# The last pair of heads of an attention and expert kernel: separate buffers, parallel copies, and slots scaled in the activation

## The chip, the cores and the metric

The kernel runs on one core of a Trainium2 chip. The metric is device time in microseconds (us), as the median of several runs. Five engines are spoken of: PE (TensorE: matrix multiply, and transposes by an identity matrix), DVE (VectorE), ACT (ScalarE), POOL (GpSimd) and SP (SyncE, which issues the transfers). Each runs its own instructions in the order written and waits for others by semaphores.

## The reference

For 4 batches and 8 heads of 768 tokens and 64 values, an attention with a window and a few global keys:

```
scores = q @ k.T / 8 - slope[h] * dist          # 96 last keys, and 8 global keys
a = exp(scores - max); a = a / (a.sum(-1) + 1e-9)
x = a @ v                                       # -> 3072 tokens x 512
logits = x @ phi                                # 3072 x 32 slots
d = exp(logits - logits.max(0)); d = d / (d.sum(0) + 1e-9)
slot_input = d.T @ x                            # 32 slots x 512
h = relu(slot_input[e] @ w1[e])                 # 8 experts, 4 slots each, 512 -> 1024
slot_out = h @ w2[e]                            # 1024 -> 512
c = softmax(logits, over slots); out = c @ slot_out
```

Dividing a slot by its sum of `d` is a scale of one row of `slot_input`. Since `relu(s * y) = s * relu(y)` for positive s, it can stand before the first expert product or in the activation behind it.

## The kernel before

The attention is done in 16 units: 4 batches, and in each 4 pairs of heads. For a unit PE makes scores, DVE adds the bias and takes a maximum, ACT takes the exponential and a float16 high part (`w_hi`), POOL and DVE the low part (`w_lo`), PE multiplies by the values (`values`, L609, 39 products a head). DVE then adds a small constant to the sums (`ev_sums`, L622), takes reciprocals (`ev_recs`, L628) and multiplies (`ev_mul`, L634, one a head). PE transposes the result (`tr`, L646: four blocks for k = 0, three for k = 1), and ACT or DVE copies the transposed parts out of PSUM (`tr_copy`, L651; `tr_copy_dve`, L655). With two units transposed, `logits` (L676) multiplies by `phi`. The last unit is 15; its own logits are made in `logits2`.

The order in which the instructions stand on every engine is a table written out by hand, `ORDER`: a list of steps with unit and head. There is no planner; what one row of the table issues stands behind what the rows ahead of it issued.

At the end of each batch the logits strip is added up (`logits_all`, L693), the running maximum over batches is updated (`strip_max`, L710 and L711) and the exponential `ex` is taken on ACT (`strip_exp`, L716). Batches 0 to 2 then turn `ex` into token rows (L732, L745), and `dispatch` (L755) multiplies it with x; `dispatch_sum` (L766) adds the product to the slot sums `sacc`.

For batch 3 that is `last_dispatch`, the stretch between the attention and the expert layer: `ex` is turned (L732) into one PSUM tile and copied (L745) into `dn`; DVE finds a factor per strip (L799 to L802, ACT L803); 14 products (L755); a product with ones (L815) for the sums; DVE divides (L816 to L818) and adds (L766); PE brings the 128 strip rows of `sacc` together into slots (L827, two pairs), and DVE copies them into `sl` (L96). Between these stand short products that nothing reads (`warm`, L542).

The expert layer begins with `hidden` (L101): 128 products of 512 columns into two banks, `hp[0]` and `hp[1]`, each step being 4 products for one block c of 128 inputs and one half n, then ACT's Relu (L119, L124). `project` (L154) and `combine` (L206) follow, whose outputs ACT and DVE copy (L211) and SP sends off (L212). Behind `hidden` SP loads the expert weights that had no room (L404), into buffers which `hidden` has read.

Two heads of a unit share one PSUM tile of two banks, `xx`, and `sc[0]` and `sc[1]` are two more such tiles; instructions on one tile wait for each other as written by the tile library.

## Time and profile before

| | us |
|---|---|
| median of 3 runs | 187.21 (186.58 to 187.63) |
| the profiled execution | 186.55 |
| its span | 184.5 |
| PE busy | 171.4 (93%) |
| DVE busy | 141.3 (77%) |
| ACT busy | 124.8 (68%) |
| POOL busy | 96.8 (52%) |

The profile is of one execution. Its span runs from the first instruction to the last; 2.05 us of the execution lie around it. Busy shares are means over stages: the attention takes the first two thirds, the stretch of `last_dispatch` begins at about 128 us, `hidden` at 134.98 us, and the last output is issued at about 178 us.

### The profile page before, as it was taken

How to read it: one execution, taken by the hardware profiler on the slowest of the kernel's cores; microseconds unless marked ns; L12 is line 12 of the kernel's file. 1: busy time of each engine (PE TensorE's matmuls, PEld its weight loads, DVE VectorE, ACT ScalarE, POOL GpSimd, SP SyncE). 2: the span in 40 equal slices, each digit the busy share in tenths (PEclk: the TensorE clock that was granted, in tenths of full speed). 3: DMA queues.
4: the chain of work that ended last, by engine and by line, in shares of the span. 5: the costliest groups of instructions: out<-in, count | busy, mean ns of one | idle time of the engine just before them, and what ended most of it. 6: DMA issues, size and time to landing. Idle time of an engine off the chain costs nothing. (4 is left out here: it accounts for less than half of the span.)

```text
span 184.5 us, 6749 instructions
## 1 busy us (share of the span) xinstructions
PE 171.4 (93%) x2811; PEld 126.4 (69%) x2811; DVE 141.3 (77%) x378; ACT 124.8 (68%) x160; POOL 96.8 (52%) x128
## 2 busy tenths in 40 slices
PE   8999899999999999999999998998899999999740
PEld 2567689797878878989788896874443256677530
DVE  5999999999999899999999999886687203345330
ACT  3399989999989999979999999942302110344330
POOL 6826689859789489797998978720010000000000
PEclk9999999999999999999999999999999999999965
DMA  6999999979989954889885599999999999979792
GB/s 197 414 413 368 413 401 380 367 220 339 378 318 361 386 195 179 313 314 358 294 338 216 167 291 400 383 380 421 415 359 311 420 401 409 372 274 400 304 362 86
DMA packets 15306, 61.41 MB, mean 333 GB/s; under 512 B 1698, under 2 KB 2850, under 8 KB 13474
## 3 DMA queue, kind: packets, MB, share of 16 engines
q1 hardware_dynamic: 15264, 60.89, 87.8%
q8 instruction: 24, 0.39, 0.8%
q14 instruction: 16, 0.13, 0.2%
q10 hardware_dynamic: 2, 0.00, 0.0%
HBM read 54.59 MB, written 6.29 MB: 330 GB/s over the span
## 5 line engine op out<-in xcount | busy, mean ns | idle before, releaser
L592 POOL TENSOR_TENSOR ph<-tb,ph 128x432 f16<-128x432 f32 x83 | 85.7, 1063 | 19.2 <-ACT ph L585 18.0
L582 ACT ACTIVATE tb<-tb,nb 128x1296 f32<-128x1296 f32 x32 | 43.7, 1374 | 0.9 <-DVE nb L578 0.8
L609 PEld LDWEIGHTS <-ph 128*128 128x128 f16 x1248 | 40.6, 97 | 4.5 <-issue 3.2
L609 PE MATMUL x<-v,ph 128*128 128x65 f16 (+1 forms) x1248 | 43.1, 193 | 0.6 <-DVE xmax L634 0.3
L585 ACT CAST ph<-tb 128x1296 f16<-128x1296 f32 x32 | 40.6, 1271 | 2.5 <-PE x L609 0.7
L557 PE MATMUL sc<-raw 64*128 64x216 f32 (+1 forms) x392 | 40.8, 340 | 0.0
L557 PEld LDWEIGHTS sc<-raw 64*128 64x128 f32 x392 | 32.3, 186 | 6.0 <-issue 3.5
L634 DVE CUSTOM_DVE_ANT_1 xn<-x,rc 120x448 f32<-120x448 f32 x32 | 18.8, 621 | 2.1 <-PE m L755 1.6
L566 DVE CUSTOM_DVE_ANT_1 tb<-sc,tt,mx 128x864 f32<-128x864 f32 x16 | 17.8, 1114 | 1.1 <-DVE mx L566 0.7
L535 DVE SCALAR_TENSOR_TENSOR v<-vt,v 128x896 f16<-128x896 f32 x14 | 16.0, 1144 | 0.0
L646 PE MATMUL m<-ident,xn 120*128 120x120 f32 x105 | 15.6, 276 | 0.2 <-DVE xmax L634 0.2
L646 PEld LDWEIGHTS m<-ident,xn 120*128 120x128 f32 x105 | 10.7, 140 | 2.7 <-issue 1.2
L101 PE MATMUL hp<-wp,sl 128*32 128x512 f32 x80 | 10.7, 593 | 0.0
L206 PE MATMUL cp<-sos,ct 32*128 32x128 f32 (+1 forms) x116 | 8.6, 343 | 1.3 <-DVE sos L193 1.1
L566 DVE CUSTOM_DVE_ANT_1 tb<-sc,xtt,mx 128x864 f32<-128x864 f32 x8 | 8.9, 1114 | 0.4 <-DVE mx L566 0.2
L592 DVE TENSOR_TENSOR ph<-tb,ph 128x432 f16<-128x432 f32 x13 | 9.1, 721 | 0.0
L566 DVE CUSTOM_DVE_ANT_1 tb<-sc,xta,mx 128x864 f32<-128x864 f32 x8 | 8.9, 1110 | 0.2
L528 ACT ACTIVATE v<-vt 128x896 f16<-128x896 f32 x9 | 8.6, 951 | 0.1
L566 DVE CUSTOM_DVE_ANT_1 tb<-sc,tt 128x864 f32<-128x864 f32 x8 | 8.4, 1051 | 0.0
L154 PE MATMUL o<-wp,ht 128*32 128x128 f32 x256 | 8.2, 275 | 0.0
L884 POOL MEMSET ht<- 128x536 f32 x1 | 0.5, 544 | 14.0 <-PE ld L827 14.0
L206 PEld LDWEIGHTS cp<-sos,ct 32*128 32x128 f32 x116 | 5.9, 192 | 2.6 <-DVE sos L193 1.5
(220 smaller groups left out, 283.4 us busy)
## 6 DMA issues: line engine op xcount, KB each, us to landing
raw<-in_qk_dram SPq DMA_DIRECT2D x14, 832.0 KB, 6.2
wp<-in_w_dram SPq DMA_DIRECT2D x10, 1024.0 KB, 8.4
wp<-in_w_dram SPq DMA_DIRECT2D x15, 512.0 KB, 9.3
vt<-in_v_dram SPq DMA_DIRECT2D x14, 448.0 KB, 5.4
tb<-in_w_dram SPq DMA_DIRECT2D x3, 1024.0 KB, 8.6
wp<-in_qk_dram SPq DMA_DIRECT2D x2, 832.0 KB, 9.6
raw<-in_w_dram SPq DMA_DIRECT2D x2, 832.0 KB, 4.6
ph<-in_w_dram SPq DMA_DIRECT2D x2, 768.0 KB, 8.9
```

What stands on the lines that cost most here:

```text
L101: self.nc.tensor.matmul(out=hp[n][32 * s:32 * s + 32, :], lhsT=slv(a, c, s), rhs=w1(4 * a + s, c // 2)[:, (c % 2) * DF + 512 * n:(c % 2) * ...
L206: nc.tensor.matmul(out=cps[b][:, w * h:w * h + w], lhsT=ct[r, P * t:P * t + P], rhs=so[r, f:f + w], start=True, stop=True)
L528: nc.scalar.activation(out=vhi[u % 2][:, :, :, 0:D], in_=vraws(u), func=AF.Copy, scale=V_SC)
L535: nc.vector.scalar_tensor_tensor(out=vlo[k].rearrange("p j i d -> p (j i) d"), in0=vraws(u).rearrange("p j i d -> p (j i) d"), scalar=V_SC ...
L557: nc.tensor.matmul(out=z[:, i, at:at + n], lhsT=r_[r, KCOL[j]:KCOL[j] + KR], rhs=r_[r, KW + KB * j:KW + KB * j + n], start=True, stop=True)
L566: nc.vector.tensor_tensor_reduce(out=tb(u)[:, :, BW * k:BW * k + BW], in0=sc[(3 * u + k) % 2][:, :, 0:BW], in1=table.unit(u % NP, k), scal ...
L582: nc.scalar.activation(out=t, in_=t, func=AF.Exp, bias=nbs[u], scale=T_SC)
L585: nc.scalar.copy(out=blocks(phi_[i])[:, :, 0:QW], in_=tb(u)[:, i].rearrange("p (s c) -> p s c", c=QW))
L592: (engine or nc.gpsimd).tensor_tensor(out=blocks(plo_[i])[:, c, 0:QW], in0=tb(u)[:, i].rearrange("p (s c) -> p s c", c=QW)[:, c], in1=bloc ...
L609: nc.tensor.matmul(out=x[:, (D + 1) * t:(D + 1) * t + d], lhsT=w[:, c:c + P], rhs=vv[:, j, i, 0:d], start=(z == 0), stop=(z == len(ops) - ...
L634: nc.vector.tensor_tensor_reduce(out=xnb[(u // 2) % 3][:, :, c:c + D], in0=xv[:, i, :, 0:D], in1=rcs.pop((u, i)).unsqueeze(2).to_broadcast ...
L646: nc.tensor.transpose(out=m[:, at:at + KB], in_=xnb[(u // 2) % 3][:, t, P * (p % 2):P * (p % 2) + P], identity=ident[0:KB, 0:KB])
```

## The change

The rows of `ORDER` at the end of unit 15 are written in another order, and `LAST_BANKS` gives the last units other PSUM banks: the second head of unit 15 gets a bank of its own in `sc[0]`, is normalised by itself (`ev_sum`, `ev_rec`, `ev_mul`) ahead of the first head, and the two turned parts of unit 15 stand in two tiles, one copied by DVE and one by ACT. Unit 14's turned parts go to the two banks of `sc[1]`. `dispatch_sum` of batch 2 moves behind the copies.

`strip_max` keeps the negative of the maximum, in one instruction. For batch 3 the sum of `ex` is a DVE reduction in place of ACT's accumulator. In `last_dispatch` `ex` is turned into two tiles and copied as two halves ahead of ACT's exponential of the factor; the 14 products stand together; two of the five `warm` calls go. The slots are not divided: `hidden` takes the reciprocal as the Relu's scale (`zn`, one number per row). Slots of the first two blocks are copied by ACT; those of the later two (`put_rest`) are made inside `hidden`, behind its first four products, and with them goes the softmax over slots on DVE.

```diff
-('values', 15, 1), ('dispatch_sum', 11), ('values', 15, 0), ('tr', 14, 1), ('tr_copy', 13, 0), ('tr_copy', 14, 1), ('ev_sums', 15), ('ev_recs', 15),
+('values', 15, 1), ('ev_sum', 15, 1), ('ev_rec', 15, 1), ('ev_mul', 15, 1), ('values', 15, 0), ('tr', 14, 1), ('tr_copy', 13, 0), ('tr', 14, 0),
...
         return view
-    def put_slots(self, sl, m, c0=0, c1=4):
+    def put_slots(self, sl, m, c0=0, c1=4, copy=None):
         n = 4 * (c1 - c0)
         out = bass.AP(tensor=sl.tensor, offset=sl.offset + 8 * 4 * c0, ap=[sl.ap[0], [P + SPE, 2], [8, n], [1, SPE]])
-        self.nc.vector.tensor_copy(out=out, in_=m.rearrange("p (cs a i) -> p a cs i", a=2, i=SPE))
+        (copy or self.nc.vector.tensor_copy)(out=out, in_=m.rearrange("p (cs a i) -> p a cs i", a=2, i=SPE))
     def hidden_part(self, hp, slv, w1, a, c, n):
...
                 start=(a == 0 and c == 0), stop=(a == 1 and c == 3), skip_group_check=True)
-    def hidden(self, ps, slv, w1, hs, ht, freed=(None, None)):
+    def hidden(self, ps, slv, w1, hs, ht, freed=(None, None), scale=1.0, rest=None):
         hp = [ps.tile([P, 512], F32, name="hp", tag="x") for _ in range(2)]
...
                 self.hidden_part(hp, slv, w1, 0, c, n)
+                if c == 0 and n == 0 and rest:
+                    rest()
         if freed[0]:
...
             freed[1]()
-        self.nc.scalar.activation(out=hs[:, 0:512], in_=hp[0], func=AF.Relu)
+        self.nc.scalar.activation(out=hs[:, 0:512], in_=hp[0], func=AF.Relu, scale=scale)
         for c in range(4):
...
             self.hidden_part(hp, slv, w1, 1, c, 1)
-        self.nc.scalar.activation(out=hs[:, 512:1024], in_=hp[1], func=AF.Relu)
+        self.nc.scalar.activation(out=hs[:, 512:1024], in_=hp[1], func=AF.Relu, scale=scale)
     HT = 2 * 32 * 8 + 24
...
     i4 = keep.tile([P, NS], F32, name="i4")
+    by_row = keep.tile([P, NS], F32, name="by_row")
     ones = keep.tile([P, P], F32, name="ones")
...
         nc.gpsimd.tensor_tensor(out=i4, in0=i4, in1=ident[:, 96:128], op=ALU.add)
+        nc.gpsimd.tensor_copy(out=by_row.rearrange("p (s j) -> p s j", s=4), in_=ident.rearrange("p (s r) -> p s r", s=4)[:, :, 0:NS // 4])
         nc.gpsimd.memset(sl, 0.0)
...
         return tbuf[u % 3]
-    LAST_BANKS = {("logits", last): (0, 0), ("tr", last, 0): (1, 0), ("tr", last, 1): (1, 1)}
+    LAST_BANKS = {("tr", last - 1, 1): sc[1][:, 1], ("tr", last - 1, 0): sc[1][:, 0], ("logits", last - 2): sc[0][:, 0],
+                  ("tr", last, 0): xx[:, 1], ("tr", last, 1): sc[1][:, 1], ("logits", last): sc[0][:, 1]}
+    def sums(u, i):
+        return sc[0][:, i] if (u, i) == (last, 1) else xx[:, i]
     def bank(key):
         if key in LAST_BANKS:
-            k, i = LAST_BANKS[key]
-            return sc[k][:, i]
+            return LAST_BANKS[key]
         return psm.tile([P, 512], F32, name="m", tag="m")
...
         vh, vl = vhi[u % 2], vlo[u % 2]
-        x = xx[:, i]
+        x = sums(u, i)
         ops = []
...
     xv = xx[0:KB, :, 0:NJ * (D + 1)].rearrange("p i (t d) -> p i t d", d=D + 1)
+    def by_query(u, i):
+        return sums(u, i)[0:KB, 0:NJ * (D + 1)].rearrange("p (t d) -> p t d", d=D + 1)
     def ev_sum(u, i):
-        nc.vector.tensor_tensor(out=rsall[:, 2 * u + i, :], in0=xv[:, i, :, D], in1=eps, op=ALU.add)
+        nc.vector.tensor_tensor(out=rsall[:, 2 * u + i, :], in0=by_query(u, i)[:, :, D], in1=eps, op=ALU.add)
     def ev_rec(u, i):
...
         nc.vector.tensor_tensor_reduce(
-            out=xnb[(u // 2) % 3][:, :, c:c + D], in0=xv[:, i, :, 0:D], in1=rcs.pop((u, i)).unsqueeze(2).to_broadcast([KB, NJ, D]), scale=1.0,
+            out=xnb[(u // 2) % 3][:, :, c:c + D], in0=by_query(u, i)[:, :, 0:D], in1=rcs.pop((u, i)).unsqueeze(2).to_broadcast([KB, NJ, D]), scale=1.0,
             scalar=-3.0e38, op0=ALU.mult, op1=ALU.max, accum_out=xmax[:, m:m + 1])
...
         if b == 0:
-            nc.vector.tensor_copy(out=new, in_=al[:, 4:5])
+            nc.vector.tensor_scalar(out=new, in0=al[:, 4:5], scalar1=-1.0, scalar2=None, op0=ALU.mult)
         else:
-            nc.vector.tensor_tensor(out=new, in0=al[:, 4:5], in1=old, op=ALU.max)
-        nc.vector.tensor_scalar(out=al[:, 1:2], in0=new, scalar1=-1.0, scalar2=None, op0=ALU.mult)
+            nc.vector.tensor_scalar(out=new, in0=al[:, 4:5], scalar1=-1.0, scalar2=old, op0=ALU.mult, op1=ALU.min)
     @of_b
...
         al = als[b]
-        nc.scalar.activation(out=ex, in_=lsb, func=AF.Exp, bias=al[:, 1:2], accum_out=al[:, 3:4])
+        new, old = state[:, b % 2:b % 2 + 1], state[:, 1 - b % 2:2 - b % 2]
+        if b < B - 1:
+            nc.scalar.activation(out=ex, in_=lsb, func=AF.Exp, bias=new, accum_out=al[:, 3:4])
+        else:
+            nc.scalar.activation(out=ex, in_=lsb, func=AF.Exp, bias=new)
         if b:
-            old = state[:, 1 - b % 2:2 - b % 2]
-            nc.scalar.activation(out=al[:, 0:1], in_=old, func=AF.Exp, bias=al[:, 1:2])
+            nc.scalar.activation(out=al[:, 0:1], in_=old, func=AF.Exp, bias=new, scale=-1.0)
     @of_b
...
             nc.vector.scalar_tensor_tensor(out=zsum, in0=zsum, scalar=al[:, 0:1], in1=al[:, 3:4], op0=ALU.mult, op1=ALU.add)
-    def to_tokens(m, x, at):
-        for k in range(2):
+    def to_tokens(m, x, at, ks=range(2)):
+        for k in ks:
             nc.tensor.transpose(out=m[0:KB, at + P * k:at + P * k + P], in_=x[:, KB * k:KB * k + KB], identity=ident)
...
     zr = keep.tile([P, 2, NS], F32, name="zr")
-    zn = keep.tile([P, NS], F32, name="zn")
+    zd = keep.tile([P, NS], F32, name="zd")
+    zn = keep.tile([P, 1], F32, name="zn")
     def last_dispatch(left, warm):
...
         for s in range(4):
-            nc.vector.tensor_reduce(out=ft[32 * s:32 * s + 32, 0:1], in_=m4, axis=AX.X, op=ALU.max)
-        nc.vector.tensor_tensor(out=ft[:, 1:2], in0=top, in1=ft[:, 0:1], op=ALU.subtract)
+            nc.vector.tensor_reduce(out=ft[32 * s:32 * s + 32, 0:1], in_=m4, axis=AX.X, op=ALU.min)
+        nc.vector.tensor_tensor(out=ft[:, 1:2], in0=ft[:, 0:1], in1=top, op=ALU.subtract)
+        nc.vector.tensor_reduce(out=als[b][:, 3:4], in_=ex, axis=AX.X, op=ALU.add)
+        strip_sum(last)
+        dns[b] = dn = wk.tile([KB, 2, P], F32, name="dn", tag="dn", bufs=1)
+        turned = [tile(), tile()]
+        for k in range(2):
+            to_tokens(turned[k], ex, -P * k, (k,))
+        for k in range(2):
+            nc.scalar.copy(out=dn[:, k], in_=turned[k][0:KB, 0:P])
         nc.scalar.activation(out=ft[:, 2:3], in_=ft[:, 1:2], func=AF.Exp)
-        strip_sum(last)
+        ms[b, "d"] = ml
+        lnat_copy(last)
         nc.vector.tensor_scalar(out=zi[:, 0], in0=i4, scalar1=ft[:, 2:3], scalar2=None, op0=ALU.mult)
         nc.vector.tensor_scalar(out=zi[:, 1], in0=zi[:, 0], scalar1=zsum, scalar2=None, op0=ALU.mult)
-        ms[b, "d"] = tile()
-        to_tokens(ms[b, "d"], ex, 0)
-        by_token_copy(last)
-        ms[b, "d"] = ml
-        lnat_copy(last)
-        warm()
-        md, mz = [tile(), tile()], tile()
-        dispatch_part(md[0], b, 0, 0, True)
+        md = [tile(), tile()]
+        for g in range(2):
+            for k in range(2):
+                dispatch_part(md[g], b, k, g, k == 0)
+        mz = tile()
         nc.tensor.matmul(out=mz[:, 0:NS], lhsT=ones, rhs=zi[:, 1], start=True, stop=True)
+        for g in range(2):
+            add_slots(b, md[g], slice(256 * g, 256 * g + 256))
+        def put(g, copy=None):
+            m = tile()
+            for c in (2 * g, 2 * g + 1):
+                nc.tensor.matmul(out=m[:, NS * c:NS * c + NS], lhsT=sacc[:, P * c:P * c + P], rhs=zi[:, 0], start=True, stop=True)
+            moe.put_slots(sl, m[:, 2 * NS * g:2 * NS * g + 2 * NS], 2 * g, 2 * g + 2, copy)
+        put(0, nc.scalar.copy)
         nc.vector.tensor_scalar(out=zr[:, 0], in0=mz[:, 0:NS], scalar1=1.0e-9, scalar2=None, op0=ALU.add)
         nc.vector.reciprocal(out=zr[:, 1], in_=zr[:, 0])
-        nc.vector.tensor_tensor(out=zn, in0=zi[:, 0], in1=zr[:, 1], op=ALU.mult)
-        dispatch_part(md[0], b, 1, 0, False)
-        for k in range(2):
-            dispatch_part(md[1], b, k, 1, k == 0)
-        for g in range(2):
-            add_slots(b, md[g], slice(256 * g, 256 * g + 256))
-        for g in range(2):
-            m = tile()
-            for c in (2 * g, 2 * g + 1):
-                nc.tensor.matmul(out=m[:, NS * c:NS * c + NS], lhsT=sacc[:, P * c:P * c + P], rhs=zn, start=True, stop=True)
-            if g == 0:
-                warm()
-            moe.put_slots(sl, m[:, 2 * NS * g:2 * NS * g + 2 * NS], 2 * g, 2 * g + 2)
+        nc.vector.tensor_tensor(out=zd, in0=zr[:, 1], in1=by_row, op=ALU.mult)
+        nc.vector.tensor_reduce(out=zn, in_=zd, axis=AX.X, op=ALU.add)
+        return lambda: put(1)
     def bcast(u):
...
     left = LeftBanks()
-    last_dispatch(left, lambda: warm_x(last))
+    put_rest = last_dispatch(left, lambda: warm_x(last))
     att.close()
...
     hs = places[6][:, 0:DF]
-    nc.vector.memset(fl, 1.0)
-    nc.vector.tensor_reduce(out=fl[0:KB, 0:1], in_=lnat, axis=AX.XY, op=ALU.min)
-    nc.vector.tensor_scalar(out=fl[0:KB, 0:1], in0=fl[0:KB, 0:1], scalar1=NEG, scalar2=None, op0=ALU.is_ge)
-    moe.softmax(lnat, cst, lnat)
+    def rest_of_slots():
+        put_rest()
+        nc.vector.memset(fl, 1.0)
+        nc.vector.tensor_reduce(out=fl[0:KB, 0:1], in_=lnat, axis=AX.XY, op=ALU.min)
+        nc.vector.tensor_scalar(out=fl[0:KB, 0:1], in0=fl[0:KB, 0:1], scalar1=NEG, scalar2=None, op0=ALU.is_ge)
+        moe.softmax(lnat, cst, lnat)
     w1_of = lambda e, half: places[where[0, e, half]]
...
         load_w([31], 0, WP // 4)
-    moe.hidden(left, Moe.slot_view(sl), w1_of, hs, ht, (reuse_first, reuse_second))
+    moe.hidden(left, Moe.slot_view(sl), w1_of, hs, ht, (reuse_first, reuse_second), zn, rest_of_slots)
     load_w([31], WP // 4, WP // 2)
```

On DVE, at the end of the attention, the rows were and are as follows (`xn_106` holds the normalised heads, `rsall` the sums, `xta` and `tt` the turned parts, `lsb` the logits strip, `sacc` the slot sums; `sc_170` and `sc_171` are `sc[0]` and `sc[1]` before, `sc_171` and `sc_172` are the same two after). Before:

```order
L766 SCALAR_TENSOR_TENSOR sacc<-sacc,al,m 128x512
L622 TENSOR_TENSOR rsall<-x,eps 120x14
L628 RECIPROCAL rc<-rsall 120x14
L634 ISA xn_106,xmax<-x,rc 120x7x64
L634 ISA xmax 120x1
...
L727 SCALAR_TENSOR_TENSOR state<-state,al 128x1 x2
L655 COPY tt<-m 128x480
L655 COPY xta<-sc_171 128x288
L693 ISA lsb,al<-sc_170,lsb 96x240
```

After:

```order
L625 TENSOR_TENSOR rsall<-sc_171,eps 120x7
L629 RECIPROCAL rc<-rsall 120x7
L644 ISA xn_106,xmax<-sc_171,rc 120x7x64
L644 ISA xmax 120x1
L625 TENSOR_TENSOR rsall<-x,eps 120x7
...
L644 ISA xn_106,xmax<-x,rc 120x7x64
...
L739 SCALAR_TENSOR_TENSOR state<-state,al 128x1 x2
L665 COPY xta<-x 128x480
L778 SCALAR_TENSOR_TENSOR sacc<-sacc,al,m 128x512
L703 ISA lsb,al<-sc_171,lsb 96x240
```

One sum and one reciprocal over both heads became one each per head, and the second head's stand first; one of the two copies went to ACT, and the addition to `sacc` stands behind the copy that is left.

On ACT, from the last turned parts to the copy of the slots (`dn` is the turned `ex`, `ft` the factor, `lnat` the logits by token, `sl` the slots). Before:

```order
L651 COPY tt<-m 128x288
L683 COPY lsb<-m 96x240
L683 COPY lsb<-m 32x48
L651 COPY xta<-sc_171 128x480
L716 ACTIVATE ex,al<-lsb,al 128x240
L719 ACTIVATE al<-state,al 128x1
L803 ACTIVATE ft<-ft 128x1
L745 COPY dn<-ld 120x256
L749 COPY lnat<-ld 120x8x32
```

After:

```order
L661 COPY tt<-sc_172 128x288
L661 COPY tt<-sc_172 128x480
L693 COPY lsb<-sc_171 96x240
L693 COPY lsb<-sc_171 32x48
L661 COPY xta<-sc_172 128x288
L729 ACTIVATE ex<-lsb,state 128x240
L731 ACTIVATE al<-state 128x1
L823 COPY dn<-ld 120x128 x2
L824 ACTIVATE ft<-ft 128x1
L761 COPY lnat<-ld 120x8x32
L96 COPY sl<-ld 128x2x8x4
```

The copies of `dn` stand ahead of the exponential `ft` and not behind it, one copy of a turned part came over from DVE, and a copy of slots was added.

On PE, from the 14 products of the last dispatch into `hidden` (`ld` is any of the small PSUM tiles, `hp` the hidden layer, `wp` weights). Before:

```order
L755 MATMUL ld<-xn_106,dn 32x256 x4
L815 MATMUL ld<-zi,ones 128x32
L755 MATMUL ld<-xn_106,dn 32x256 x10
L827 MATMUL ld<-zn,sacc 128x32 x2
L542 LDWEIGHTS ident
L542 MATMUL x<-ident 128x256
...
L827 MATMUL ld<-zn,sacc 128x32 x2
L101 MATMUL hp<-wp_83,sl 32x512
```

After:

```order
L767 MATMUL ld<-xn_106,dn 32x256 x14
L834 MATMUL ld<-zi,ones 128x32
L841 MATMUL ld<-zi,sacc 128x32 x2
L101 MATMUL hp<-wp_83,sl 32x512
L101 MATMUL hp<-wp_84,sl 32x512
L101 MATMUL hp<-wp_85,sl 32x512
L101 MATMUL hp<-wp_86,sl 32x512
L841 MATMUL ld<-zi,sacc 128x32 x2
L101 MATMUL hp<-wp_83,sl 32x512
```

The second pair of slot products moved behind the first four products of `hidden`, and the short products that nothing reads are gone from here.

## Rows read from the trace of the kernel before

**Rows 1.** Busy time by stretch: each engine's busy us (instructions), granted clock, DMA share, GB/s.
```profile
130.00:135.00 5.00, 4.35 (x49) 2.79 (x49) 3.18 (x14) 0.98 (x5) 0.00 (x0) 1.00 1.01 409
135.00:140.00 5.00, 5.00 (x49) 1.56 (x52) 3.97 (x6) 0.67 (x1) 0.54 (x1) 1.00 1.00 329
175.00:180.00 5.00, 2.12 (x28) 1.64 (x28) 2.08 (x6) 1.71 (x6) 0.00 (x0) 0.64 0.98 365
```

**Rows 2.** PE's longest wait after 134 us: who, for what, total, times, longest.
```profile
PE cp L206 <- DVE sos L193: 1.1, 2, 0.9
```

**Rows 3.** Timeline, end of unit 15's heads: start, us, engine, line, operands, [idle before, releaser].
```profile
121.09 1.64 DVE L592 TENSOR_TENSOR ph<-tb,ph 128x432 f16<-128x432 f32 x3
121.23 2.52 PE L609 MATMUL x<-v,ph 128*128 128x65 f16 x78 [0.30 <-DVE xmax L634]
...
123.79 0.17 DVE L622 TENSOR_TENSOR rsall<-x,eps 120x14 f32<-120x14 f32 x1 [0.40 <-PE x L609]
124.27 0.62 DVE L634 CUSTOM_DVE_ANT_1 xn<-x,rc 120x448 f32<-120x448 f32 x1
```

**Rows 4.** Timeline, the last turns, their copies and the logits.
```profile
123.59 0.91 PE L646 MATMUL m<-ident,xn 120*128 120x120 f32 x7
125.52 0.94 PE L646 MATMUL sc<-ident,xn 120*128 120x120 f32 x7
125.66 0.57 ACT L683 COPY lsb<-m 96x240 f32<-96x240 f32 x2 [1.14 <-PE m L676]
125.75 0.65 DVE L655 COPY tt<-m 128x480 f32<-128x480 f32 x1
...
126.50 0.46 DVE L655 COPY xta<-sc 128x288 f32<-128x288 f32 x1
126.98 0.56 ACT L651 COPY xta<-sc 128x480 f32<-128x480 f32 x1 [0.75 <-DVE xta L655]
127.60 0.61 PE L676 MATMUL sc<-xta,phis 128*32 128x240 f32 x8 [0.54 <-ACT xta L651]
```

**Rows 5.** Timeline, the strip's maximum and exponential, batches 3 and 2.
```profile
129.09 0.16 DVE L710 TENSOR_TENSOR state<-al,state 128x1 f32<-128x1 f32 x1
129.29 0.15 DVE L711 TENSOR_SCALAR al<-state 128x1 f32<-128x1 f32 x1
129.47 0.49 ACT L716 ACTIVATE ex<-lsb,al 128x240 f32<-128x240 f32 x1 [1.93 <-DVE al L711]
129.87 0.19 ACT L716 ACTIVATION_READ_ACCUMULATOR ex<-lsb,al 128x1 f32 x1
...
115.60 0.50 ACT L716 ACTIVATE ex<-lsb,al 128x240 f32<-128x240 f32 x1 [0.36 <-DVE al L711]
```

**Rows 6.** Timeline, from the turned `ex` to the first dispatch product; and a smaller ACT copy.
```profile
130.12 0.44 PE L732 MATMUL ld<-ident,ex 128*120 128x128 f32 x2 [0.23 <-ACT ex L716]
130.84 0.20 ACT L803 ACTIVATE ft<-ft 128x1 f32<-128x1 f32 x1 [0.60 <-DVE ft L802]
130.95 0.35 ACT L745 COPY dn<-ld 120x256 f32<-120x256 f32 x1
131.36 0.64 PE L755 MATMUL ld<-xn,dn 120*32 120x256 f32 x8 [0.54 <-ACT dn L745]
...
165.46 0.27 ACT L183 COPY ows<-o 128x128 f32<-128x128 f32 x1 [0.21 <-PE o L154]
```

**Rows 7.** Timeline: dispatch of batch 2 in one piece, slot products, their copy, `hidden`, a Relu.
```profile
118.45 1.93 PE L755 MATMUL m<-xn,dn 120*32 120x256 f32 x28
...
133.69 0.63 PE L827 MATMUL ld<-zn,sacc 128*128 128x32 f32 x4
134.36 0.23 DVE L96 COPY sl<-ld 128x64 f32<-128x64 f32 x1
134.45 0.60 PE L827 MATMUL ld<-zn,sacc 128*128 128x32 f32 x4
134.98 7.49 PE L101 MATMUL hp<-wp,sl 128*32 128x512 f32 x66
```

**Rows 8.** Last weights, issued 154 to 155 us (KB, us to landing); their use on PE.
```profile
wp<-in_w_dram SPq DMA_DIRECT2D x2, 512.0 KB, 9.5
...
168.95 2.83 PE L154 MATMUL o<-wp,ht 128*32 128x128 f32 x96
```

2 lines of the change are left out of this document (1 added, 1 removed).

## The prediction

> **What bounds the kernel now.** I read the page's busy shares and slices first, then busy time by stretch, then PE's waits, then the timeline of the stretch that the change edits. PE is busy 93% of the span, but what counts is where it waits. From 135 us on PE is busy 5.00 of 5 us [rows 1], and up to the end its longest kind of wait is 1.1 us in total, for a DVE copy; no wait for a transfer is in the list [rows 2]. The last weights are issued before 155 us and land 9.5 us later, by 164.5; the products at 168.95 are the first that need them, 4.5 us later [rows 8]. So the expert layer is PE's own work, and the kernel ends as much earlier as `hidden`, at 134.98 us, begins earlier. Ahead of it, from 121 to 135 us, no engine is the bound: PE has 4.35 of 5 us even with its unread products counted, DVE 3.18, ACT 0.98 [rows 1]. There the time is a chain of short steps from engine to engine, and the change edits that chain.
>
> **The change part by part.** Times of before are on the profile's clock.
>
> A, heads, turns and logits. Before, the sums wait for both heads' products, 123.79 [rows 3], and the turns of unit 15 begin at 125.52 [rows 4]. After, the second head's sums need only the first 39 of the 78 products, half of 2.52 us, so by 122.5. DVE is free of its three low parts at 122.73 (121.09 + 1.64 [rows 3]). From sum to multiply is 0.48 us (123.79 to 124.27) and the multiply takes 0.62 [rows 3], so each head is 1.10: the second head done at 123.83, the first at 124.93. PE meanwhile turns unit 14 and makes the logits of unit 13. Its products end up to 0.30 earlier (the wait in [rows 3] goes, since the second head has a bank of its own), at about 123.45; the seven turns take 0.91, the logits at most the 1.16 us from 124.50 to ACT's start at 125.66 [rows 4], and both overlap by some tenths at their ends. PE is thus ready for the turns of unit 15 at about 125.0, which is the later of the two; gain 0.5. Then, before: turns 0.94, DVE's copy, ACT's copy that idled 0.75 for DVE's, logits at 127.60, that is 2.08 us from 125.52 [rows 4]. After: four turns, about 0.6 of the 0.94, then DVE's copy of 480 columns, 0.65 as in [rows 4], and 0.1 for two handovers: 126.35. ACT's side is its queue: from 124.3 four copies, two of turned parts (0.56 for 480 columns [rows 4], and 0.4 for 288, between that and the 0.27 for 128 [rows 6]), the strip (0.57 [rows 4]) and one more of 288, which is 126.25. The two meet. Logits begin at 126.35 in place of 127.60: -1.25. Bounds: -0.8 if ACT's handovers add up, -1.45 if PE is ready when DVE is. The addition to `sacc`, moved behind the copy, has the 0.61 us of logits as cover and a little more.
>
> B, one DVE instruction less ahead of the exponential: 129.09 to 129.29 [rows 5], -0.20.
>
> C, no accumulator read: the exponential ends at 129.96, the read at 130.06, and PE turns at 130.12 [rows 5, 6], so PE waited for the read: -0.10. Bounds: 0 if it did not, -0.24 if without an accumulator the exponential is as short as the copy of 256 columns, 0.35 [rows 6]. The sum of `ex` becomes a DVE reduction, in E. I take -0.10, since the duration of the exponential itself has a row. The Trainium skill, "ScalarE: Activation LUTs" ("What ACT_TABLE_LOAD costs"), gives an ACTIVATE with one per-partition operand 280 ns and 0.833 ns a column, an estimate of 0.48 us for these 240. The row's 0.49 bears that out, so by the rule the exponential keeps its length and the sum below stands; by the copy's length it would be 0.14 more gain.
>
> D, from the turned `ex` to the dispatch. Before 130.12 to 131.36, 1.24 us, because the copy of `dn` stood on ACT behind the factor's exponential, which idled 0.60 for DVE [rows 6]. After: one turn (between half of 0.44 and all, say 0.33), one copy of 128 columns, 0.27 [rows 6], and 0.11 for two handovers: 0.71. -0.53; bounds -0.35 and -0.6. The second half is copied while PE does the first four products.
>
> E, from the dispatch to `hidden`. Before 131.36 to 134.98, 3.62 us. After: 14 products in one piece 1.93, slot pair 0.63 [rows 7], the ones product between them about 0.2 (a pair takes 0.63), ACT's copy 0.25 (DVE's is 0.23, ACT's of 128 columns 0.27 [rows 6, 7]), handovers 0.1, less 0.2 because a row's duration holds the drain that the next product covers: 2.9. -0.72; bounds -0.4 and -0.9. Beside it DVE must have the first half of `sacc`: before, the chain from the maximum to both factors took 2.5 us (129.09 to about 131.6); with a reduction of 240 columns (0.2 to 0.5) it takes 2.9, then 0.5 for the addition, ready about 131.2 on the new clock, where PE arrives at 131.4. That cover is 0.2 us, no more.
>
> F, the second slot pair inside `hidden`: +0.53 (134.45 to 134.98 [rows 7]). Its copy stands on DVE behind the four small instructions of the division, and block c = 1 waits for it. By the steps above the division is done near 132.8 and the pair near 133.3; the copy of 0.23 lands at about the time PE wants it. +0.05, bounds 0 and +0.2.
>
> G, batches 0 to 2: one DVE instruction less each. At 115.60 ACT had idled 0.36 for it [rows 5]; -0.1, bounds 0 and -0.2. POOL's new copy at the start and ACT's Relu with a scale from memory I cost at nothing. The Relu's result is turned only behind the next three blocks of `hidden`, and ACT has 0.67 of 5 us to do there [rows 1]; without that cover it would cost what it grows by. The softmax on DVE begins earlier with the rest.
>
> Sum: -1.25 - 0.20 - 0.10 - 0.53 - 0.72 + 0.53 + 0.05 - 0.10 = -2.32 us. The execution profiled took 186.55 (184.5 and 2.05 around it), which would become 184.2; the median shown is 187.21, 0.66 more, and the forecast is for such a median: 184.9. With all bounds at their good ends the gain is 3.1, at their bad ends 1.0: 184.1 to 186.2, and some tenths either way for the spread of runs.
>
> **The rivals.** R1, the change does less than it says in A. PSUM waits go by tile: the logits of unit 13 and the second head share `sc[0]`, the turns of unit 15 stand behind these logits, and ACT has five copies where it had three. If they run strictly one after another, A gives 0.5 and the time is 185.7. For it: ACT's copy idled 0.75 for a copy from another bank of the same tile [rows 4]. Against: the two copies of unit 15 now read two tiles.
>
> R2, transfers set the end: their share is 1.0 from 130 to 140 us [rows 1]. Then an earlier `hidden` waits for weights, and the time stays at 187.2. Against: the 4.5 us of slack [rows 8], and that SP's reloads wait for products of `hidden` and move with them.
>
> R3, slower: the clock. The granted clock is 1.00 (2.4 GHz) from 130 to 140 us with PE busy 4.35 of 5, and it fell to half (1.2 GHz) in 175 to 180, 0.64 in the mean, where PE had 2.12 of 5 [rows 1]. Two of five groups of unread products go, and the waits for `dn` and for ACT's slot copy stay. If the clock falls there, each us of PE work done at half costs one more us, and from 2.3 us on the kernel is slower; with 4 us of `hidden`, 187.2 - 2.3 + 4 = 188.9. Against: PE's own work in the stretch is packed closer than before.
>
> **How the numbers follow.** Forecast 0.78, R1 0.12, R2 0.05, R3 0.05. The range takes the forecast's 184.1 to 186.2 with the spread of runs and R1: 183.6 to 186.5, leaving out R2, R3 and some tails, 0.16. Half a per cent, 0.94 us, is about what runs of this kernel can tell from no change. Faster by more: 0.76 of the forecast and 0.10 of R1, 0.86; within: 0.02, 0.02 and 0.04 of R2, 0.08; slower: R3 and a hundredth of R2, 0.06.
>
> **What would show it.** A: the logits of unit 15 about 1.25 us earlier, with DVE's and ACT's copies of its parts side by side. B, C, D: the first dispatch product about 2.1 us earlier, and ACT's exponential of the factor behind both `dn` copies. E, F: the first product of `hidden` about 2.9 us earlier, and from its second block on 2.3. From there to the end the distances as before. I am wrong if PE waits inside `hidden` for the second slot copy, if the tail waits for weights, or if the granted clock in 125 to 140 us is under 1.00.

## The result, and the profile after

The changed kernel takes 185.18 us (median of 6 runs, 184.79 to 185.42) beside 186.72 of the kernel before (6 runs): ratio 0.9894 (95%: 0.9872 to 0.9915), so faster by 0.8 to 1.3%. The ratios, here and among the experiments, leave out executions over 1.5% longer than the fastest of the same kernel (one of e10, 187.12 us, and one of e11, 189.76 us). Forecast were 184.9 us and a gain of 2.3. The time lies inside the range, and the gain, 1.54 between the medians, is smaller than the sum. That the time came within 0.3 us is in part luck: the forecast set out from 187.21, the median of the first three runs of before, and six runs have 186.72. Judge the prediction by the gain.

One thing has to be cleared away before two timelines are laid side by side. In the changed kernel's profile PE's and DVE's work stands some 0.35 us *later* than before from the first scores to 118 us. The timeline of PE and DVE, before, at the start (start, us, engine, line, operands, [idle before, releaser]):

```profile
4.08 2.27 PE L546 MATMUL x<-const-bfloat16-1.0 128*1 128x512 bf16 x6
6.28 1.73 PE L557 MATMUL sc<-raw 64*128 64x216 f32 x16
...
7.32 1.06 DVE L566 CUSTOM_DVE_ANT_1 tb<-sc,tt 128x864 f32<-128x864 f32 x1
```

The same place in the changed kernel:

```profile
4.07 2.62 PE L553 MATMUL x<-const-bfloat16-1.0 128*1 128x512 bf16 x6
6.63 1.73 PE L564 MATMUL sc<-raw 64*128 64x216 f32 x16
...
7.67 1.06 DVE L573 CUSTOM_DVE_ANT_1 tb<-sc,tt 128x864 f32<-128x864 f32 x1 [0.42 <-PE sc L564]
```

And in a second execution of the very same changed kernel (e9 below):

```profile
3.87 1.46 PE L553 MATMUL x<-const-bfloat16-1.0 128*1 128x512 bf16 x6
5.26 1.73 PE L564 MATMUL sc<-raw 64*128 64x216 f32 x16
...
7.16 1.04 DVE L573 CUSTOM_DVE_ANT_1 tb<-sc,tt 128x864 f32<-128x864 f32 x1
```

The six unread products at the start take 1.46 us in one execution and 2.62 in another, and the first scores, with DVE's first biased scores, follow. That is chance of an execution, not the change. By 118 us, ahead of all that the change edits at the end of the attention, the same DVE row stands like this in before, the changed kernel and e9, in this order:

```profile
118.24 0.16 DVE L622 TENSOR_TENSOR rsall<-x,eps 120x14 f32<-120x14 f32 x1
118.60 0.16 DVE L632 TENSOR_TENSOR rsall<-x,eps 120x14 f32<-120x14 f32 x1
118.27 0.16 DVE L632 TENSOR_TENSOR rsall<-x,eps 120x14 f32<-120x14 f32 x1
```

So distances below are taken from there on: "net" is the difference of two start times less the difference that the two profiles already have in this row (0.36 for before and after; PE's rows there give 0.33, so a net value is good to some 0.03).

Heads, turns and logits of unit 15, changed kernel, where [rows 3, 4] stood (timeline):

```profile
122.42 1.48 PE L616 MATMUL x<-v,ph 128*128 128x65 f16 x39
...
123.73 0.91 PE L656 MATMUL sc<-ident,xn 120*128 120x120 f32 x7
124.40 0.62 DVE L644 CUSTOM_DVE_ANT_1 xn<-x,rc 120x448 f32<-120x448 f32 x1
125.00 0.58 PE L686 MATMUL sc<-xtt,phis 128*32 128x240 f32 x6
125.52 0.63 PE L656 MATMUL x<-ident,xn 120*128 120x120 f32 x4
125.66 0.56 ACT L693 COPY lsb<-sc 96x240 f32<-96x240 f32 x2
...
126.19 0.66 DVE L665 COPY xta<-x 128x480 f32<-128x480 f32 x1 [0.77 <-PE x L656]
126.49 0.40 ACT L661 COPY xta<-sc 128x288 f32<-128x288 f32 x1 [0.27 <-PE sc L656]
126.90 0.64 PE L686 MATMUL sc<-xta,phis 128*32 128x240 f32 x8
```

The two copies of unit 15 now overlap, and ACT's 0.75 us of idling for DVE's copy is gone. The last logits start at 126.90 in place of 127.60. PE has no wait from 121 to 128 us: the last logits stand directly behind PE's own turns and first logits, and the two copies end just then, at 126.85 and 126.89. From there to the dispatch, where [rows 5, 6] stood:

```profile
128.39 0.21 DVE L720 TENSOR_SCALAR state<-al,state 128x1 f32<-128x1 f32 x1
128.63 0.49 ACT L729 ACTIVATE ex<-lsb,state 128x240 f32<-128x240 f32 x1 [1.74 <-DVE state L720]
129.18 0.44 PE L744 MATMUL ld<-ident,ex 128*120 128x128 f32 x2
129.54 0.43 ACT L823 COPY dn<-ld 120x128 f32<-120x128 f32 x2 [0.23 <-PE ld L744]
129.86 1.93 PE L767 MATMUL ld<-xn,dn 120*32 120x256 f32 x28 [0.24 <-ACT dn L823]
130.13 0.20 ACT L824 ACTIVATE ft<-ft 128x1 f32<-128x1 f32 x1 [0.15 <-DVE ft L815]
```

PE's wait ahead of the dispatch is 0.24 us, not 0.54, and ACT makes the factor behind the copies. From the dispatch into `hidden` ([rows 7]):

```profile
131.85 0.48 DVE L778 SCALAR_TENSOR_TENSOR sacc<-sacc,al,ld 128x256 f32<-128x256 f32 x1 [0.17 <-PE ld L767]
131.96 0.61 PE L841 MATMUL ld<-zi,sacc 128*128 128x32 f32 x4
132.61 0.21 ACT L96 COPY sl<-ld 128x64 f32<-128x64 f32 x1 [2.01 <-PE ld L841]
132.88 1.07 PE L101 MATMUL hp<-wp,sl 128*32 128x512 f32 x8 [0.30 <-ACT sl L96]
133.08 0.19 DVE L848 TENSOR_REDUCE zn<-zd 128x1 f32<-128x32 f32 x1
133.87 0.63 PE L841 MATMUL ld<-zi,sacc 128*128 128x32 f32 x4
134.43 1.06 PE L101 MATMUL hp<-wp,sl 128*32 128x512 f32 x8
134.54 0.22 DVE L96 COPY sl<-ld 128x64 f32<-128x64 f32 x1 [1.27 <-PE ld L841]
```

Read the PE rows downward: slot pair, 0.30 us of waiting for ACT's copy, the first four products (8 records), the second pair at 133.87, and `hidden` goes on at 134.43. Busy time by stretch (us, PE, PEld, DVE, ACT, POOL, granted clock, DMA share, GB/s), beside [rows 1]:

```profile
130.00:135.00 5.00, 4.70 (x54) 2.48 (x53) 3.17 (x14) 0.68 (x3) 0.38 (x1) 1.00 1.01 404
135.00:140.00 5.00, 5.00 (x52) 1.45 (x47) 3.75 (x5) 1.06 (x1) 0.16 (x1) 1.00 1.02 401
175.00:180.00 5.00, 0.61 (x12) 0.42 (x12) 0.94 (x3) 0.72 (x3) 0.00 (x0) 0.71 0.89 322
```

From 130 to 140 us the clock stays at 1.00, and PE is full from 135 to 140. PE's longest kind of wait behind 130 us is the one of [rows 2], with the same 1.1 us, so the tail only moves. The products on the first reloaded tile, before and after:

```profile
141.89 0.60 PE L101 MATMUL hp<-raw,sl 128*32 128x512 f32 x2
140.48 0.60 PE L101 MATMUL hp<-raw,sl 128*32 128x512 f32 x2
```

That is -1.41, net -1.77. In e9 they stand at 140.15, 1.74 earlier than before, and there next to nothing has to be subtracted (118.27 against 118.24). The outputs up to the one issued at 173.86 move by 1.40 too, the last one by 1.60; the span shrank by 1.2, since from the last issue to the end of the span it took 7.3 us and 6.9 before. That last stretch takes from 6.3 to 7.3 us in the fourteen profiles and has no part in the argument.

### The profile page after: what moved, and what is told of

The parts are those of the page before. It is cut to its first block, busy times and chain, and to the rows that moved or that the text cites. A ratio compares the mean times of both kernels' runs of the same rounds, so it can differ in the third digit from the quotient of the medians.

```text
span 183.3 us, 6741 instructions
## 1 busy us (share of the span) xinstructions
PE 170.7 (93%) x2805; PEld 125.8 (69%) x2805; DVE 141.4 (77%) x376; ACT 125.7 (69%) x162; POOL 97.2 (53%) x129
## 4 chain that ended last, share of the span: by engine, by line
## 5 line engine op out<-in xcount | busy, mean ns | idle before, releaser
L616 PE MATMUL x<-v,ph 128*128 128x65 f16 (+1 forms) x1209 | 42.0, 193 | 0.4 <-POOL ph L599 0.2
L644 DVE CUSTOM_DVE_ANT_1 xn<-x,rc 120x448 f32<-120x448 f32 x31 | 18.3, 622 | 2.1 <-PE m L767 1.7
L656 PE MATMUL m<-ident,xn 120*128 120x120 f32 x98 | 14.7, 276 | 0.2 <-DVE state L737 0.2
L656 PEld LDWEIGHTS m<-ident,xn 120*128 120x128 f32 x98 | 10.0, 141 | 2.7 <-issue 1.5
L599 DVE TENSOR_TENSOR ph<-tb,ph 128x432 f16<-128x432 f32 x13 | 9.6, 766 | 0.0
L156 PEld LDWEIGHTS o<-wp,ht 128*32 128x32 f32 x256 | 6.6, 110 | 1.4 <-issue 1.0
```

The source lines that it names most:

```text
L156: nc.tensor.matmul(out=o[32 * s:32 * s + 32, o0:o0 + w], lhsT=ht[:, k:k + 32], rhs=w2(4 * a + s, half)[:, at:at + w], start=(a == 0 and c ...
L599: (engine or nc.gpsimd).tensor_tensor(out=blocks(plo_[i])[:, c, 0:QW], in0=tb(u)[:, i].rearrange("p (s c) -> p s c", c=QW)[:, c], in1=bloc ...
L616: nc.tensor.matmul(out=x[:, (D + 1) * t:(D + 1) * t + d], lhsT=w[:, c:c + P], rhs=vv[:, j, i, 0:d], start=(z == 0), stop=(z == len(ops) - ...
L644: nc.vector.tensor_tensor_reduce(out=xnb[(u // 2) % 3][:, :, c:c + D], in0=by_query(u, i)[:, :, 0:D], in1=rcs.pop((u, i)).unsqueeze(2).to_ ...
L656: nc.tensor.transpose(out=m[:, at:at + KB], in_=xnb[(u // 2) % 3][:, t, P * (p % 2):P * (p % 2) + P], identity=ident[0:KB, 0:KB])
```

## The experiments

All were timed beside the kernel before. The ratio is to it, with its 95% interval.

| kernel | median us (lowest to highest), runs | ratio |
|---|---|---|
| e1 heads only | 185.86 (185.72 to 185.94), 6 | 0.9941 (0.9923 to 0.9958) |
| e2 rest only | 186.45 (185.60 to 187.26), 12 | 0.9978 (0.9962 to 0.9995) |
| e3 pair ahead | 184.89 (184.47 to 186.09), 6 | 0.9901 (0.9875 to 0.9927) |
| e4 products ahead | 184.72 (184.35 to 185.89), 6 | 0.9877 (0.9857 to 0.9898) |
| e5 factor first | 185.92 (185.22 to 186.59), 8 | 0.9941 (0.9918 to 0.9965) |
| e6 sign as before | 185.45 (185.15 to 186.33), 6 | 0.9917 (0.9887 to 0.9947) |
| e7 division ahead | 185.81 (185.72 to 187.21), 12 | 0.9947 (0.9926 to 0.9967) |
| e8 dispatch split | 185.09 (184.20 to 186.69), 6 | 0.9910 (0.9874 to 0.9945) |
| e9 changed again | 185.18 (184.81 to 186.08), 6 | 0.9913 (0.9887 to 0.9938) |
| e10 products ahead again | 184.58 (184.19 to 187.12), 6 | 0.9882 (0.9858 to 0.9906) |
| e11 no unread | 185.70 (184.67 to 189.76), 6 | 0.9925 (0.9898 to 0.9952) |
| e12 no unread again | 184.81 (184.60 to 186.44), 6 | 0.9901 (0.9867 to 0.9935) |

**e1 and e2, part A alone and all but part A.**

```
 before.py                                   (e1)
-LAST_BANKS = {("logits", last): (0, 0), ...
+LAST_BANKS = {..., ("tr", last, 0): xx[:, 1], ...     and the new ORDER, sums, by_query
 after.py                                    (e2)
-ORDER = ... ('ev_sum', 15, 1), ('ev_rec', 15, 1), ('ev_mul', 15, 1) ...
+ORDER = ... ('ev_sums', 15), ('ev_recs', 15) ...      and the old LAST_BANKS
```

> The kernel before with part A alone: the new order of the last two pairs, their banks, and the heads normalised apart; everything behind the logits is as before. Theory 1 (each part shortens its own piece of the chain and the pieces add): in the two profiles the logits of unit 15 end 1.05 us earlier if both are set to the same start of the first scores, so the time is that of before less 1.05, 185.7 us. Rival (what A gains is absorbed behind it, since DVE's factor or the transfers set the start of the expert layer): no change, 186.7. On the start: in the changed kernel's profile the first scores of PE begin 0.35 us later (6.63 against 6.28). If that is chance of one execution, it falls either way in the profiles of these runs; if the new edits to the early batches or POOL's new copy cause it, this kernel, which has neither, starts at 6.28.

> The changed kernel with part A undone: the old order and banks, one sum and one reciprocal for both heads; the rest of the change stands. Theory 1: 185.18 + 1.05 = 186.2 us. Rival (A is absorbed by what follows): 185.2. Start of the first scores in the profile: 6.63 if the edits outside A cause the late start, either value if it is chance.

In e1 the last logits start at 126.93, where before had 127.60, and its profile lay 0.37 later ahead of them: net -1.04. In e2 they start at 127.27, net 1.01 later than in the changed kernel. Both signs of the test agree, and e1's median, 1.02 under that of before (186.88), says the same; e2's, 1.27 above the changed kernel's, says it less sharply, with a scatter of 1.7 us. A is worth 1.0 us and nothing behind it takes it back: at the first reloaded tile e1 is net 1.05 ahead of before and e2 net 0.75, which together are the 1.77 of the changed kernel but for 0.03. The start of the first scores, 5.60 and 5.41, speaks for chance.

**e3 and e4, the second slot pair ahead of the layer.**

```
 after.py                                    (e3)
-        return lambda: put(1)
+        put(1)
 after.py                                    (e4)
-        put(0, nc.scalar.copy)
+        m0, m1 = slots(0), slots(1)
+        moe.put_slots(sl, m0, 0, 2, nc.scalar.copy)
...
-        return lambda: put(1)
+        return lambda: moe.put_slots(sl, m1, 2, 4)
```

> The changed kernel with the second slot pair and its copy made ahead of the expert layer, behind the division, as before; nothing is made inside the layer's first product. Theory 1 (PE's idle time ahead of the layer is what the pair fills, but the copy on DVE now stands behind the division, which ends at 133.27, so the first product can begin at about 133.6, where in the changed kernel PE had done as much by 133.56): no change, 185.2 us. Rival 2 (making the pair inside costs its whole 0.68 us, which it would not cost outside): 184.5. Rival 3 (inside it is free): 185.9.

> The changed kernel with the second pair's products right behind the first pair's, where PE idles 0.30 us for ACT's slot copy, and only its copy left inside the first product of the layer. Theory 1: PE's idle time of 0.30 goes under the pair (0.56), the first product begins at about 133.15 in place of 132.88, but nothing stands in it any more, so from the second block on all is 0.35 us earlier: 184.8 us. Rival (the pair then waits for the second half of the slot sums on DVE, done at 132.33, or the copy stands too late for the block that needs it): no change, 185.2.

I had expected no gain of e3, on the idea that the layer's first product waits for DVE's copy behind the division. It doesn't: in e3 `hidden` starts at 132.24, and that copy at 132.47. The blocks that need the second half come later. From the pair on, e3 is net 0.63 earlier than the changed kernel (-0.71 ahead of it, -1.34 behind), e4 net 0.64 (+0.61 and -0.03). So rival 2 holds for e3 in the trace: made inside the layer, the pair costs its 0.6 us; made outside it costs next to nothing. e3's median, 0.29 under the changed kernel's, lies between its forecasts and decides less; e4's, 0.46 under, is near its theory's 184.8, though by the trace that theory had too little, 0.35 for 0.64.

**e9 and e10, the changed kernel and e4 side by side.**

> The changed kernel itself once more, beside the two that follow on one chip. Theory (its first profile began the scores at 6.63, later than eight of the nine other profiles, and DVE's first biased scores at 7.67 where those of the undelayed ones stand at 7.1; that is chance of an execution): the profile begins DVE's first biased scores near 7.1, the second block of the expert layer stands near 133.9 in place of 134.43, and the time is 185.0, with a scatter of half a us. Rival (the edits cause the late start): again 7.67, 185.2.

> The kernel with the second pair's products right behind the first pair's, now beside the changed kernel on one chip. Theory (making the pair inside the layer costs the 0.6 us by which the two kernels' profiles differ from the pair on): 0.6 us under the changed kernel run beside it, some 184.4 to 184.6. Rival (the 0.6 us is given back in the tail, by transfers): equal within 0.2.

```
 no edit: the two kernels once more, on one chip
```

The medians are 185.18 and 184.58; the traces of these two give net 0.64. The timeline of e10 from the ones product on:

```profile
131.04 0.41 PE L834 MATMUL ld<-zi,ones 128*128 128x32 f32 x2
131.29 1.06 PE L841 MATMUL ld<-zi,sacc 128*128 128x32 f32 x8
131.94 0.21 ACT L96 COPY sl<-ld 128x64 f32<-128x64 f32 x1 [2.02 <-PE ld L841]
132.28 3.21 PE L101 MATMUL hp<-wp,sl 128*32 128x512 f32 x28
132.50 0.21 DVE L96 COPY sl<-ld 128x64 f32<-128x64 f32 x1
```

ACT's copy now lies under the second pair and PE waits for nothing. Of the 0.6, 0.30 is that wait; the rest is that two pairs in one piece last 0.99 us from start to start (131.29 to 132.28) where apart they last 0.61 and 0.56, and that the first block, broken off, took 0.99 (132.88 to 133.87) in place of some 0.86. On the start the theory held (e9: 7.16), but e9's execution lost 0.2 of the 0.5 again by 103 us, so that the layer's second block stood at 134.10 and not at 133.9, and the rest in the last outputs, and took the same 185.42 us as the first. So a late start alone does not decide the time. e10 is the best version that was run; it beats the kernel before by 0.9 to 1.4%, and the changed one by the 0.6 us of medians and traces.

**e5, e6, e7, one step undone each.**

```
 after.py                                    (e5)
-        for k in range(2):
-            nc.scalar.copy(out=dn[:, k], in_=turned[k][0:KB, 0:P])
         nc.scalar.activation(out=ft[:, 2:3], in_=ft[:, 1:2], func=AF.Exp)
+        nc.scalar.copy(out=dn.rearrange("p k s -> p (k s)"), in_=turned[0:KB, 0:2 * P])
 after.py                                    (e6): strip_max, strip_exp as before, without
-        nc.vector.tensor_reduce(out=als[b][:, 3:4], in_=ex, axis=AX.X, op=ALU.add)
 after.py                                    (e7): ones, division, zd = zi * zr behind four products
+        dispatch_part(md[0], b, 0, 0, True)
+        nc.tensor.matmul(out=mz[:, 0:NS], lhsT=ones, rhs=zi[:, 1], start=True, stop=True)
```

> The changed kernel with step D undone: the turned exponentials go to one bank and are copied at once, and on ACT that copy stands behind the factor's exponential again. Theory 1 (the copy waits for DVE's chain to the factor, which ends at 130.10 on the changed kernel's clock: exponential 0.13, copy of 256 columns 0.35, so the dispatch begins at about 130.65 in place of 129.86): 0.8 us later, 186.0 us. Rival (the step is worth the 0.56 by which the two profiles differ there): 185.7. Rival 2 (the start of the dispatch decides nothing, DVE's slot sums set the start of the layer): 185.2.

> The changed kernel with the sign and the accumulator as before in all four batches: maximum and negation in two DVE instructions, the sum of the exponentials read from ACT's accumulator. Theory 1: the first turn of the last exponentials begins 0.25 us later (0.15 for DVE's instruction, 0.10 for the read), the early batches cost nothing: 185.4 us, and from the first scores to 118 us the profile keeps its distance to that of the changed kernel. Rival (the early batches' instruction is on the path, 0.1 each): 185.7. Rival 2 (DVE's own reduction of 240 columns, 0.40, which goes away here, was as long on the path as what it replaced): 185.0 to 185.2.

> The changed kernel with the division ahead of the slots, as before: the ones product behind the first four dispatch products, the divided factor as the right operand of the slot products, Relu unscaled; the second pair stays inside the layer. Theory 1 (DVE's chain to both factors ends at 131.16, and the ones product, in PE's queue ahead of the other 24 dispatch products, holds them until then: 131.4 + 1.64, the slots begin at 133.05 in place of 131.96): 1.1 us later, 186.3 us. Rival (the parts add: the step is worth the 0.60 by which the two profiles differ there): 185.8.

e5: the dispatch starts at 130.10, net 0.78 later, and the median is 0.74 higher. PE's row shows the wait for the copy, the 0.24 of the changed kernel grown to 1.03:

```profile
130.10 0.64 PE L767 MATMUL ld<-xn,dn 120*32 120x256 f32 x8 [1.03 <-ACT dn L822]
```

That is more than the 0.56 between the two profiles. From the start of DVE's maximum to the dispatch, e5 takes 2.26 us (127.84 to 130.10), the kernel before 2.27 (129.09 to 131.36) and the changed kernel 1.47 (128.39 to 129.86). So with D undone ACT's copy waits again for DVE's chain to the factor, and that chain is no shorter than before: what B and C gain ahead of the turn, 0.24, is lost as well. e6: the last exponentials are turned net 0.25 later, and the median is 0.27 higher. From DVE's first biased scores to the row at 118 us e6 takes 110.90 us and the changed kernel 110.93, so the early batches give nothing that can be seen; B and C together give 0.25. e7: PE stands still for the factors,

```profile
129.30 0.64 PE L767 MATMUL ld<-xn,dn 120*32 120x256 f32 x8 [0.25 <-ACT dn L823]
130.65 0.41 PE L831 MATMUL ld<-zi,ones 128*128 128x32 f32 x2 [0.72 <-DVE zi L828]
130.99 1.50 PE L767 MATMUL ld<-xn,dn 120*32 120x256 f32 x20
```

and `hidden` starts at 133.35, net 1.0 later. From the start of the maximum to the ones product e7 takes 2.83 us (127.82 to 130.65), the kernel before 2.84 (129.09 to 131.93): with the ones product among those of the dispatch, what B, C and D gain is lost in the wait for the factors. The median is only 0.63 higher, which is what the rival said, with a scatter of 1.5 us. The ratios of e7 and of the changed kernel, each to the kernel before beside it, differ by 0.53%, or 1.0 us, as the trace says; I go by the trace.

**e8, half a dispatch moved to where PE idles.**

```
 products ahead
-    ... ('dispatch', 11) ... ('logits2', 15), ...
+    ... ('dispatch', 11) [g = 0 only] ... ('logits2', 15), ('dispatch2', 11) [g = 1], ...
+        nc.scalar.activation(out=ex, in_=ex, func=AF.Copy, accum_out=als[b][:, 3:4])
```

> The kernel with the second pair's products ahead of the layer, and on top of it 14 of the 28 dispatch products of batch 2 (0.96 us of PE) moved from 120 us, where PE works without a gap, to behind the last logits, where it idles; the sum of their half of the slots moves with them, ACT makes the sum of the last exponentials, and the ones product stands behind the slot products. Theory 1 (from 118 to 127.5 us PE's own work is the bound, which is why part A gave 1.05 and not 1.25): everything from the last logits on 0.9 us earlier, 183.8 us. Rival (DVE's and POOL's low parts of unit 15 set the pace there): no more than the 184.7 of the kernel that it is built on. Rival 2 (the transfer into the last slot buffer, now later in the queue, makes the tail wait): slower than 184.7.

The theory fell: 185.09, not better than e4. PE reached unit 15's heads 0.9 us earlier and waited there for POOL:

```profile
119.69 0.50 PE L616 MATMUL sc<-v,ph 128*128 128x65 f16 x11
121.01 1.03 PE L616 MATMUL sc<-v,ph 128*128 128x65 f16 x28 [0.82 <-POOL ph L599]
```

POOL's three low parts, 3.62 us, end at 120.95, and in the changed kernel PE arrives just when they are done. That stretch has two bounds at once; PE's share alone does not show it. Behind it the layer began net 0.37 later than in e4: 0.09 of it stands at the dispatch already, since PE's queue made the turn of the last exponentials late, and 0.28 comes in the slot products, whose second pair starts at 132.01, behind DVE's second addition to `sacc` (131.39 to 131.87).

**e11 and e12, the last unread products left out.**

```
 after.py, last_dispatch
-        warm()
-        warm()
         strip_max(last)
...
         to_tokens(ml, lsb, 2 * P)
-        warm()
```

> The changed kernel without the three groups of unread products that are left between the last logits and the dispatch. Theory (the groups lie in PE's idle time, and PE has work enough there that the granted clock stays at 1.00): no change against the changed kernel beside it, 185.0 to 185.2, clock 1.00 from 125 to 140 us. Rival (the third rival of the prediction, drawn one step further: without them the granted clock falls to half behind the idle time): part of the dispatch and of the expert layer at half clock, one more us for each us of it, 187 to 189.

> The kernel without the three groups of unread products once more, since its first six runs spread from 184.67 to 189.76 us where its profile, of the run of 184.67, kept the clock at 1.00. Theory (the groups cost and give nothing; the long run was chance): median 185.2, no run over 186.5. Rival (without them the clock falls behind the idle time in some executions): again one or more of the runs at 187 or above with a mean clock under 0.970.

In both profiles the granted clock is 1.00 from 125 to 140 us though PE is less busy, and from the dispatch of batch 2 to the layer's second block they take 15.65 and 15.66 us, the changed kernel 15.65: on this stretch the groups cost and give nothing. The stretch from 127.5 to 130 in e11 (columns as above):

```profile
127.50:130.00 2.50, 1.55 (x19) 0.86 (x23) 2.17 (x16) 1.55 (x6) 0.00 (x0) 1.00 1.02 427
```

One run of e11 took 189.76 us at a mean clock of 0.956; its trace was not taken, the six runs of e12 show none like it (highest 186.44), and whether the missing products had a part in it stays open. The medians, 185.70 and 184.81, lie on either side of the changed kernel's 185.18. In all profiles taken the third rival is false.

## Why the prediction was right, and where its sizes were off

The mechanism is as forecast in the main: the chain from unit 15's sums to `hidden` is what the time hangs on, the tail moves with it, and no transfer or clock stood in the way. Net at the layer's second block (and at 140.48) the profiles differ by 1.77 us, where the sum had 2.32. By its terms:

- **A**, -1.25 forecast, -1.06 measured (-1.04 by e1, -1.01 by e2), inside its bounds. The step "PE is thus ready at about 125.0" came out at 125.16 net: PE's turns and logits of unit 13 follow each other without a gap, and I had let them overlap by a little more. From there to the last logits I had 1.35 us, four turns, DVE's copy and two handovers, and 1.38 was measured. That this fits is a coincidence in part: PE needs the same 1.38 (125.52 to 126.90) for its seven turns and the first half of the logits, which the sum did not count, so shorter copies alone would have gained nothing more. R1 is false: the copies of unit 15 run side by side.
- **B and C**, -0.30 forecast, -0.24 between the profiles and -0.25 by e6. B gave 0.14 of its 0.20 (from the maximum to ACT's exponential 0.38 before, 0.24 after), since the one instruction that is left is longer; C gave its 0.10 (from the exponential to the turn 0.65 and 0.55). The exponential without an accumulator lasted 0.49 us, as with one, so PE had waited for the read alone. The estimate of 0.48 from the Trainium skill, "ScalarE: Activation LUTs" ("What ACT_TABLE_LOAD costs"), agrees with the row's 0.49.
- **D**, -0.53 forecast, -0.56 between the profiles.
- **E**, -0.72 forecast, -0.60 measured (3.02 us from the dispatch to `hidden`, I had 2.9). I had taken 0.2 off the dispatch's 1.93 for its drain; the ones product follows after 1.86, so 0.07 of it was there. The ones product took 0.24, not 0.2.
- **F**, +0.58 forecast, +0.68 measured. The copy cost nothing: it ends at 134.76 and `hidden` had no wait for it. But I took the place of the pair as given. e3, e4 and e10 show that nearly the whole term, some 0.63, could have been saved, because PE's wait in E and the pair in F cover each other.
- **G**, -0.10 forecast, 0 measured: this is the step that failed outright. From the first biased scores to the row at 118 us it took 110.92 us before and 110.93 after. ACT had idled 0.36 us for that instruction at 115.60, but nothing on the path waited for ACT there. PE's turn of batch 2's exponentials before, the same turn after, and ACT behind its exponential after:

```profile
116.26 0.42 PE L732 MATMUL m<-ident,ex 128*120 128x128 f32 x2
116.63 0.39 PE L744 MATMUL m<-ident,ex 128*120 128x128 f32 x2
116.53 1.27 ACT L592 CAST ph<-tb 128x1296 f16<-128x1296 f32 x1 [0.24 <-PE x L616]
```

PE turns them without a wait in both, net at the same time; ACT, done sooner, now waits 0.24 us for PE. An idle time that names a releaser is a price only where somebody waits for the engine that idled.

The shortfall of 0.55 is A's 0.19, E's 0.12, F's 0.10, G's 0.10, B's 0.06 and D's 0.03 the other way. R2 fell with the unchanged tail. The terms do not simply add: undone alone, D costs 0.78 and E 1.0, more than their shares of the gain, since with one of them missing ACT or PE waits for DVE's factors again and the gains ahead of that wait are lost.

## What to carry to other kernels

When a step puts a short wait on the bounding engine (here 0.30 us for a slot copy), look for work of the same engine that is ready and is to be done later anyway, and put it there, not behind the wait. Price a removed instruction only where its engine's idle time is somebody's wait, and undo steps one at a time: a step's worth beside the others may be larger than its share. Before two traces are compared, subtract what they already differ by ahead of the edit.

## What the runs showed that I had not expected

Six equal products on constant data at the start of PE's work last from 1.46 to 2.62 us in executions of one and the same kernel, though the granted clock of 3 to 7 us reads 1.00 in the profiles of before and of the changed kernel; what makes the difference is not shown. DVE's first biased scores feel it only when the scores begin late: they stand at 7.08 to 7.17 us in the eleven profiles where the scores begin by 5.88, and at 7.32, 7.42 and 7.67 where these begin at 6.28, 6.37 and 6.63. From there to 118 us most profiles take 110.8 to 111.1 us, but e1's takes 111.5 and e4's 111.8; what holds them up is not shown, and it is why single times say less here than net distances. A product that reads one half of a buffer starts before the copy into its other half has run (132.24 and 132.47 in e3, 132.28 and 132.50 in the rows of e10).
